# The opening of an attention-and-MLP kernel: halves of 256 queries, silu on GpSimd, and c on another queue

## The chip, the cores and the metric

One NeuronCore of a Trainium2 chip runs the kernel; the other cores are idle. The metric is the device time of one execution in microseconds (us), from ten runs. A profiled execution gives a trace: every engine's instructions with start and duration. The engines are PE (TensorE: matmuls, with weight loads shown apart as PEld), DVE (VectorE), ACT (ScalarE), POOL (GpSimd) and SP (SyncE, which here only issues transfers). A DMA transfer is issued by an instruction in the queue of SP, ACT or POOL, and the data moves on the core's 16 DMA engines. "Bank" is one of the eight 2 KB-per-partition banks of PSUM into which PE writes.

## The reference

The kernel computes one transformer block with adaptive layer norm. With `c` of 512 values, `w_mod` of 512 x 3072, `x` of 2048 x 512, 32 query heads of 128, 8 key/value heads and a window of the last 512 keys:

```
mod = silu(c) @ w_mod                       # six rows of 512: sa, ca, ga, sb, cb, gb
h   = layernorm(x) * (1 + ca) + sa
q   = h @ wq                                # 32 heads of 128
p   = softmax(q @ k[-512:].T / sqrt(128))   # 4 query heads share one k and v head
x   = x + ga * ((p @ v[-512:]) @ wo)
h   = layernorm(x) * (1 + cb) + sb
x   = x + gb * (relu(h @ w1) @ w2)          # w1: 512 x 1792
```

Inputs and output are bfloat16.

## The kernel before

The 2048 queries are taken in four blocks of 512 (QB), each of four tiles of 128 rows. A unit is one head of one block, so there are 128 units. A unit's work on PE is four matmuls for q (K = 512 in four chunks, called cc in the code), four for the scores, sixteen for p times v. ScalarE copies q out of PSUM (line 1493) and takes the exponential of the scores (line 1501); VectorE normalises the result (lines 1511 and 1512). Output projections and, in the end, the MLP fill PE in between.

The order of work on each engine is the order of the calls in the source. A small recorder (`kb.op`) notes for each operation what it reads and writes and works out the semaphore waits; every engine then runs its own list strictly in order. Nothing is scheduled at run time, so an instruction that waits holds up all that stand behind it on its engine or queue.

The change touches only the opening, which prepares the first block (lines 1567 to 1628). It goes like this:

- Transfers (1567 to 1575). SP's queue issues tiles 0 and 1 of x, then c as a 4 x 128 array, the first half of the modulation weights for sa and ca (`wm0`, chunks cc 0 and 1), query weights, keys (with a transposing transfer), values. ScalarE's queue issues tiles 2 and 3 of x, the second half of those weights (`wm1`, chunks 2 and 3), and the query weights of heads 0 and 1.
- GpSimd (1576 to 1581) sets constants and builds the identity matrix for transposes.
- PE (1583 to 1585) runs 7 dummy matmuls on ones (`warm`, into bank psW), transposes c to a column (`silu_exp`, line 1425), and runs 9 more. ScalarE takes exp(-c) from it (1426).
- Layer norm. VectorE takes mean and variance of tiles 0 to 2 (1377, 1378); ScalarE does the same for tile 3 with sums (1587 to 1590). GpSimd raises variance plus epsilon to the power -0.5 for two tiles at a time (`rstd_pow`, 1596). VectorE then finishes the silu in three small steps (`silu_mul`, 1430 to 1432) and normalises tiles 0 to 2 (1388); ScalarE normalises tile 3 (1609, 1610).
- The modulation columns (`mod_cols_mm`, 1434 to 1443): sa and ca are needed with one value per partition, so 32 matmuls with a single moving column give 8 columns of 128 values in bank psQ. They run column by column, the four chunks cc of each in turn, 16 before and 16 after the transposes of tile 0. VectorE copies the columns out, adding 1 to the four of ca, in two operations (1447, 1448).
- PE transposes the other tiles (`ln_tposes`, 1400 to 1404) with 1, 2 and 3 dummy matmuls behind them (1621). All tiles land in two banks, two chunks in each.
- `ln_mod_ps` (1406 to 1418) applies factor and shift, 512 queries at a time: chunks 0 and 1 on VectorE, 2 and 3 on ScalarE. Then q of units 0 and 1 (`q_mms`, 1487 to 1493), into banks psQ and 5, and from there on the steady loop (1657 to 1668).

Two lines that the change replaces, the order of the products and the place where SP gets c:

```
for c2 in range(DC):
    for cc in range(DC):
...
dma(c_row[:, :], c[0].rearrange("(c p) -> c p", p=P), "c", writes=[R_c])
```

Of the kernel before, what the change touches and what calls it, by code (L numbers as in the profile page):

```python
# [1198 lines left out]
def build_fast(nc, es, top, A_x, A_k_cache, A_v_cache, A_wq, A_wo, B_x, B_w1, B_w2, c, w_mod, out, flag):  # L1199
    P = 128  # L1200
    _, Sq, D = A_x.shape
    _, G, Sk, Dh = A_k_cache.shape
# [5 lines left out]
    QB = 512  # L1208
# [3 lines left out]
    DC = D // P  # L1212
# [3 lines left out]
    scale = float(Dh) ** -0.5  # L1216
# [21 lines left out]
    hT = [T(f"hT{i}", [P, DC, QB]) for i in range(2)]  # L1238
# [11 lines left out]
    xn = T("xn", [P, TPB, D])  # L1250
# [5 lines left out]
    ones = T("ones", [P, P])  # L1256
    c_row = T("c_row", [DC, P])
    s3 = T("s3", [P, 4], F32)
    sc_bf = T("sc_bf", [P, DC])
    sc_f = T("sc_f", [P, DC], F32)  # L1260
    tmp = T("tmp", [P, DC], F32)
# [51 lines left out]
    R_moda, R_modb, R_ga, R_gb = Res("moda"), Res("modb"), Res("ga"), Res("gb")  # L1313
    R_pr = [R_ga] + RL("pr", 2) + [R_gb]
    R_st, R_mv, R_rstd = RL("st", NT), RL("mv", NT), RL("rstd", NT)
    R_s3, R_eps = Res("s3"), Res("eps")
    R_rinv, R_vmax, R_chk, R_good, R_flag = Res("rinv"), Res("vmax"), Res("chk"), Res("good"), Res("flag")
    R_h1 = [RL(f"h1_{i}_", FC) for i in range(2)]
# [30 lines left out]
    def wm_res(sl, cc):  # L1349
        return R_wm[cc // (DC // 2)] if sl < 2 else R_wm[sl]  # L1350
# [15 lines left out]
    def mm(out_ap, lhsT, rhs, start, stop, reads, bk, signal):  # L1366
        kb.op(PE, lambda e: e.matmul(out_ap, lhsT, rhs, start=start, stop=stop), reads=reads, group_writes=[R_b[k] for k in bk], signal=signal)  # L1367
# [18 lines left out]
    def ln_norm(t):  # L1386
        b, tl = t // TPB, t % TPB
        kb.op(DVE, lambda e: e.tensor_scalar(xn[:, tl, :], x_sb[:, t, :], mv[:, t, 0:1], rstd[:, t:t + 1], op0=ALU.subtract, op1=ALU.mult),
              reads=[R_x[t], R_mv[t], R_rstd[t]], writes=[R_xn[tl]])
# [9 lines left out]

    def ln_tposes(tl, bks):  # L1400
        for cc in range(DC):
            bk = bks[cc // 2]
# [3 lines left out]
    def ln_mod_ps(bks, dst, R_dst, which):  # L1406
        o, r = (0, R_moda) if which == 1 else (2 * DC, R_modb)
        for k in range(2):
            for half, eng in ((0, DVE), (1, ACT)):
                cc = half * 2 + k  # L1410
                src = bank[bks[half]].bitcast(BF)[:, k * 512:(k + 1) * 512]
                sc, sh = modc[:, o + DC + cc:o + DC + cc + 1], modc[:, o + cc:o + cc + 1]
                if eng is DVE:
                    kb.op(DVE, lambda e, src=src, sc=sc, sh=sh, cc=cc: e.tensor_scalar(dst[:, cc, :], src, sc, sh, op0=ALU.mult, op1=ALU.add),
                          reads=[R_b[bks[half]], r], writes=[R_dst[cc]])
                else:
                    kb.op(ACT, lambda e, src=src, sc=sc, sh=sh, cc=cc: e.activation(dst[:, cc, :], src, ACTF.Identity, bias=sh, scale=sc),
                          reads=[R_b[bks[half]], r], writes=[R_dst[cc]])

    CC_ORDER = (0, 2, 1, 3)  # L1420
    QA = 2

    def silu_exp(bk):
        cT = bank[bk].bitcast(BF)[:, 0:DC]
        kb.op(PE, lambda e: e.transpose(cT, c_row[:, :], ident[0:DC, 0:DC]), reads=[R_c, R_ident], group_writes=[R_b[bk]])
        kb.op(ACT, lambda e: e.activation(tmp[:, :], cT, ACTF.Exp, scale=-1.0), reads=[R_b[bk]], writes=[R_tmp])

    def silu_mul(bk):
        cT = bank[bk].bitcast(BF)[:, 0:DC]
        kb.op(DVE, lambda e: e.tensor_scalar(tmp[:, :], tmp[:, :], 1.0, None, op0=ALU.add), reads=[R_tmp], writes=[R_tmp])  # L1430
        kb.op(DVE, lambda e: e.reciprocal(tmp[:, :], tmp[:, :]), reads=[R_tmp], writes=[R_tmp])  # L1431
        kb.op(DVE, lambda e: e.tensor_tensor(sc_bf[:, :], cT, tmp[:, :], op=ALU.mult), reads=[R_tmp, R_b[bk]], writes=[R_sc])  # L1432

    def mod_cols_mm(which, bk):
        fs = []
        for idx, sl in enumerate((0, 1) if which == 0 else (3, 4)):
            for c2 in range(DC):
                for cc in range(DC):
                    last = idx == 1 and c2 == DC - 1 and cc == DC - 1
                    fs.append(lambda sl=sl, c2=c2, cc=cc, col=idx * DC + c2, last=last: mm(  # L1440
                        bank[bk][:, col:col + 1], wm[sl][:, cc, c2 * P:(c2 + 1) * P], sc_bf[:, cc:cc + 1],
                        cc == 0, cc == DC - 1, [R_sc, wm_res(sl, cc)], [bk], last))
# [43 lines left out]

    def q_mms(u, bk=QBK):
        b, h = units[u]
        order = CC_ORDER if u < QA else range(DC)
        for i, cc in enumerate(order):  # L1490
            mm(bank[bk], wq_sb[:, cc, h * Dh:(h + 1) * Dh], hT[b % 2][:, cc, :], i == 0, i == DC - 1,
               [R_wq[h], R_hT[b % 2][cc]], [bk], i == DC - 1)
# [102 lines left out]
    def rstd_pow(lo, hi):  # L1595
        kb.op(POOL, lambda e: e.tensor_tensor(rstd[:, lo:hi], rstd[:, lo:hi], cst[:, 0:1].to_broadcast([P, hi - lo]), op=ALU.pow),
              reads=R_rstd[lo:hi] + [R_cst], writes=R_rstd[lo:hi])

    ln_stat(0)
    ln_stat(1)  # L1600
    rstd_add(0, 2)
# [8 lines left out]
    kb.op(ACT, lambda e: e.activation(xn[:, t3, :], x_sb[:, t3, :], ACTF.Identity, scale=rstd[:, t3:t3 + 1], bias=s3[:, 3:4]),  # L1610
          reads=[R_x[t3], R_rstd[t3], R_s3], writes=[R_xn[t3]])
# [249 lines left out]
```

## Time and profile before

| What | Value |
|---|---|
| median of 10 runs | 561.61 us (561.34 to 562.2) |
| profiled execution, its own time | 561.49 us |
| its span, first to last instruction | 559.8 us |
| PE busy | 550.1 us, 98% |
| ACT busy | 350.3 us, 63% |
| DVE busy | 252.7 us, 45% |
| POOL busy | 52.1 us, 9% |
| granted TensorE clock | 1.000 |

The profiled execution took 561.49 us, of which 1.69 lie outside the span. In the timeline each row gives the start and the length in us, the engine, the line of the source, the operation, output and input with their shapes, how often, and in square brackets how long the engine had been idle and what ended the idle time. A row with "x16" stands for sixteen instructions of one group and the length covers them all. In the chain of waits each row is one step of the chain that ended last: start, length, engine, tile and line.

The opening's stages in the profile before, each with its start in us:

| Start | Stage |
|---|---|
| 4.74 | first statistics on VectorE, when x has landed (line 1377) |
| 4.75 | weight load for the transpose of c on PE, when c has landed (1425) |
| 8.05 | first normalisation on VectorE (1388) |
| 8.19 | first modulation product on PE |
| 9.41 | modulation columns copied out (1447) |
| 10.75 | factor and shift applied (1414, 1417) |
| 11.44 | first matmul for q |
| 12.68 | q of unit 0 copied out (1493) |
| 13.42 | first matmul for scores |

### The profile page before, as it was taken

How to read it: one execution, taken by the hardware profiler on the slowest of the kernel's cores; microseconds unless marked ns; L12 is line 12 of the kernel's file. 1: busy time of each engine (PE TensorE's matmuls, PEld its weight loads, DVE VectorE, ACT ScalarE, POOL GpSimd, SP SyncE). 2: the span in 40 equal slices, each digit the busy share in tenths (PEclk: the TensorE clock that was granted, in tenths of full speed). 3: DMA queues.
4: the chain of work that ended last, by engine and by line, in shares of the span. 5: the costliest groups of instructions: out<-in, count | busy, mean ns of one | idle time of the engine just before them, and what ended most of it. 6: DMA issues, size and time to landing. Idle time of an engine off the chain costs nothing.

```text
span 559.8 us, 9653 instructions
## 1 busy us (share of the span) xinstructions
PE 550.1 (98%) x4057; PEld 315.0 (56%) x4132; DVE 252.7 (45%) x550; ACT 350.3 (63%) x453; POOL 52.1 (9%) x46
## 2 busy tenths in 40 slices
PE   7999999999999999999999999999999999999998
PEld 3565555555555555555555555555555654444444
DVE  3455555553546544335445443333354448321134
ACT  5986666666666666666666666666666644432500
POOL 1000022004410000033000000332000000000000
PEclk9999999999999999999999999999999999999999
DMA  9896764413214144352452422211214110200001
GB/s 270 238 213 169 144 161 59 114 39 76 40 38 76 39 70 120 57 133 58 94 95 57 75 40 39 38 39 38 39 39 76 39 30 0 45 33 23 21 30 47
DMA packets 113309, 42.67 MB, mean 76 GB/s; under 512 B 93928, under 2 KB 112104, under 8 KB 113256
## 3 DMA queue, kind: packets, MB, share of 16 engines
q1 hardware_dynamic: 112024, 40.82, 34.5%
q10 hardware_dynamic: 1232, 1.15, 0.6%
q8 instruction: 33, 0.54, 0.4%
q14 instruction: 20, 0.16, 0.1%
HBM read 18.35 MB, written 2.10 MB: 37 GB/s over the span
## 4 chain that ended last, share of the span: by engine, by line
PE 97%; issue 1%; DMA 1%; DVE 1%
PE psS L1367 28%; PE psO L1367 27%; PE psQ L1367 23%; PE psW L1367 19%; DMA x<-in_A_x_dram 1%; DVE st L1377 0%; PE psS L1370 0%; DVE mv L1378 0%; DVE rstd L1593 0%; DVE PT L1691 0%; DVE PT L1693 0%; DVE tmp L1431 0%; DVE sc_bf L1432 0%; DVE tmp L1430 0%
## 5 line engine op out<-in xcount | busy, mean ns | idle before, releaser
L1501 ACT ACTIVATE PT<-psS 128x1024 bf16<-128x1024 f32 x256 | 262.7, 1028 | 126.9 <-PE psS L1367 126.9
L1367 PE MATMUL psS<-qT,kT 128*128 128x512 bf16 x510 | 151.4, 379 | 0.1
L1367 PEld LDWEIGHTS psO<-v,PT 128*128 128x128 bf16 x2048 | 126.6, 98 | 30.2
L1367 PE MATMUL psO<-v,PT 128*128 128x129 bf16 x2048 | 137.0, 220 | 0.0
L1367 PE MATMUL psQ<-hT,wq 128*128 128x512 bf16 x505 | 130.2, 379 | 0.2
L1511 DVE RECIPROCAL rinv<-psO 128x4 f32<-128x4 f32 x128 | 23.4, 183 | 229.1 <-PE psO L1367 229.1
L1367 PE MATMUL psW<-wo,oT 128*128 128x512 bf16 x452 | 118.1, 379 | 3.1
L1512 DVE TENSOR_TENSOR o<-psO,rinv 128x512 bf16<-128x512 f32 x128 | 88.5, 691 | 4.7 <-DVE rinv L1511 0.2
L1367 PEld LDWEIGHTS psQ<-hT,wq 128*128 128x128 bf16 x508 | 49.6, 98 | 60.7 <-issue 0.5
L1367 PEld LDWEIGHTS psS<-qT,kT 128*128 128x128 bf16 x512 | 49.5, 98 | 58.9 <-ACT PT L1501 0.7
L1493 ACT ACTIVATE qT<-psQ 128x512 bf16<-128x512 f32 x127 | 75.3, 593 | 0.5 <-PE psQ L1367 0.5
L1680 ACT ACTIVATE wq<-psS 128x512 bf16<-128x512 f32 x56 | 33.4, 597 | 49.4 <-PE psS L1367 49.4
L1367 PEld LDWEIGHTS psW<-wo,oT 128*128 128x128 bf16 x512 | 44.9, 98 | 32.9 <-DVE acc L1534 1.2
L1534 DVE TENSOR_TENSOR acc<-psW,acc 128x512 f32<-128x512 f32 x48 | 33.2, 691 | 6.7 <-PE psW L1367 6.7
L1367 PE MATMUL psO<-wmw,wq 128*128 128x512 bf16 (+1 forms) x164 | 32.7, 352 | 0.3
L1537 POOL TENSOR_TENSOR acc<-acc,gaf 128x512 f32<-128x512 f32 x12 | 15.6, 1303 | 146.8 <-DVE acc L1534 139.7
L1383 POOL TENSOR_TENSOR rstd<-rstd,cst 128x4 f32<-128x4 f32 x7 | 7.2, 1026 | 218.3 <-DVE rstd L1382 218.3
L1691 DVE TENSOR_TENSOR PT<-psO,gbf 128x512 f32<-128x512 f32 (+1 forms) x12 | 7.5, 624 | 40.4 <-PE psO L1367 40.4
L1367 PE MATMUL psS<-h2T,wmw 128*128 128x512 bf16 x110 | 25.2, 379 | 0.1
L1367 PEld LDWEIGHTS psO<-wmw,wq 128*128 128x128 bf16 x168 | 15.4, 98 | 16.5
L1367 PE MATMUL psS<-hT,wmw 128*128 128x512 bf16 x110 | 24.4, 379 | 0.1
L1377 DVE BATCH_NORM_STATS2 st<-x 128x6 f32<-128x512 bf16 x31 | 21.1, 681 | 4.7 <-DMA x<-in_A_x_dram 4.7
(77 smaller groups left out, 189.1 us busy)
## 6 DMA issues: line engine op xcount, KB each, us to landing
wo<-in_A_wo_dram SPq DMA_DIRECT2D x4, 1024.0 KB, 5.8
wq<-in_A_wq_dram SPq DMA_DIRECT2D x7, 512.0 KB, 5.1
wmw<-in_B_w_dram SPq DMA_DIRECT2D x14, 256.0 KB, 3.0
wmw<-in_w_mod_dram SPq DMA_DIRECT2D x5, 512.0 KB, 4.9
oT<-o SPq DMA_TRANSPOSE x128, 2.4
out_dram<-PT SPq DMA_DIRECT2D x15, 128.0 KB, 1.7
x<-in_A_x_dram SPq DMA_DIRECT2D x3, 512.0 KB, 4.6
v<-in_A_v_cache_dram SPq DMA_DIRECT2D x8, 128.0 KB, 4.2
```

The source lines that it names most:

```text
L1367: kb.op(PE, lambda e: e.matmul(out_ap, lhsT, rhs, start=start, stop=stop), reads=reads, group_writes=[R_b[k] for k in bk], signal=signal)
L1377: kb.op(DVE, lambda e: e.bn_stats(st[:, t, :], x_sb[:, t, :]), reads=[R_x[t]], writes=[R_st[t]])
L1383: kb.op(POOL, lambda e: e.tensor_tensor(rstd[:, sl], rstd[:, sl], cst[:, 0:1].to_broadcast([P, hi - lo]), op=ALU.pow), reads=R_rstd[sl] + ...
L1493: kb.op(ACT, lambda e: e.activation(qT[u % NQT][:, :], bank[bk], ACTF.Copy), reads=[R_b[bk]], writes=[R_qT[u % NQT]])
L1501: kb.op(ACT, lambda e: e.activation(PT[u % NPT][:, pr * 2:pr * 2 + 2, :], s_ps[pr][:, :, :], ACTF.Exp, scale=scale), reads=[R_b[pr * 2], R ...
L1511: kb.op(DVE, lambda e: e.reciprocal(rinv[:, u, :], o_ps[:, :, P]), reads=[R_b[5], R_b[6]], writes=[R_rinv])
L1512: kb.op(DVE, lambda e: e.tensor_tensor(o_sb[u % NOS][:, :, :], o_ps[:, :, 0:P], rinv[:, u, :].unsqueeze(2).to_broadcast([P, TPB, P]), op=A ...
L1534: kb.op(DVE, lambda e: e.tensor_tensor(acc[:, tl, :], bank[WBK], acc[:, tl, :], op=ALU.add), reads=[R_b[WBK], R_acc[tl]], writes=[R_acc[tl]])
L1537: kb.op(eng, lambda e: e.tensor_tensor(acc[:, tl, :], acc[:, tl, :], gaf[:, :], op=ALU.mult), reads=[R_acc[tl], R_ga], writes=[R_acc[tl]])
L1680: kb.op(ACT, lambda e: e.activation(h1T[b % 2][:, fc, :], bank[bk], ACTF.Relu), reads=[R_b[bk]], writes=[R_h1[b % 2][fc]], pre=all_events( ...
L1691: kb.op(DVE, lambda e: e.tensor_tensor(yt[i][:, c0:c1], bank[bk][:, c0:c1], gbf[:, c0:c1], op=ALU.mult), reads=[R_b[bk], R_gb], writes=[R_ ...
```

## The change

It does the following, all in the opening:

- c is issued by GpSimd's queue, behind the identity matrix, instead of by SP's.
- The silu moves from VectorE to GpSimd: minimum with 1e38 and plus 1, power -1, times c. As GpSimd doesn't read PSUM here, ScalarE copies the transposed c to SBUF (`c_f`) behind the exponential.
- Tile 3 is normalised by GpSimd in one operation instead of by ScalarE in two. Tile 2 is normalised by VectorE behind the first two tiles and before the modulation columns are copied out.
- The 32 modulation products run by chunk cc, so that the first 16 need only `wm0` and the other 16 only `wm1`. They form a single accumulation in bank psQ. They are copied out by one addition of a constant (`m01`: four zeros, four ones).
- The dummy matmuls behind the transposes of tiles 1 to 3 are gone; those up to the modulation products stay.
- The transposed tiles land in separate banks for tiles 0, 1 and tiles 2, 3 (`TB`). Factor, shift and q of units 0 and 1 are done in halves of 256 queries: five of these passes on VectorE, three on ScalarE.

```diff
@@ order of the modulation products, and their way out
-        for idx, sl in enumerate((0, 1) if which == 0 else (3, 4)):
-            for c2 in range(DC):
-                for cc in range(DC):
...
+        for cc in range(DC):
+            for sl in (0, 1):
+                for c2 in range(DC):
+                    last = sl == 1 and c2 == DC - 1 and cc == DC - 1
...
-        kb.op(DVE, lambda e: e.tensor_copy(modc[:, mo:mo + DC], bank[bk][:, :DC]), reads=[R_b[bk]], writes=[r])
-        kb.op(DVE, lambda e: e.tensor_scalar(modc[:, mo + DC:mo + 2 * DC], bank[bk][:, DC:2 * DC], 1.0, None, op0=ALU.add), reads=[R_b[bk]], writes=[r])
+        kb.op(DVE, lambda e: e.tensor_tensor(modc[:, mo:mo + 2 * DC], bank[bk][:, :2 * DC], m01[:, :], op=ALU.add), reads=[R_b[bk], R_m01], writes=[r])
@@ silu
-    def silu_mul(bk):
-        cT = bank[bk].bitcast(BF)[:, 0:DC]
-        kb.op(DVE, lambda e: e.tensor_scalar(tmp[:, :], tmp[:, :], 1.0, None, op0=ALU.add), reads=[R_tmp], writes=[R_tmp])
-        kb.op(DVE, lambda e: e.reciprocal(tmp[:, :], tmp[:, :]), reads=[R_tmp], writes=[R_tmp])
-        kb.op(DVE, lambda e: e.tensor_tensor(sc_bf[:, :], cT, tmp[:, :], op=ALU.mult), reads=[R_tmp, R_b[bk]], writes=[R_sc])
+        kb.op(ACT, lambda e: e.activation(c_f[:, :], cT, ACTF.Copy), reads=[R_b[bk]], writes=[R_cf])
+
+    def silu_mul():
+        kb.op(POOL, lambda e: e.tensor_scalar(tmp[:, :], tmp[:, :], 1e38, 1.0, op0=ALU.min, op1=ALU.add), reads=[R_tmp], writes=[R_tmp])
+        kb.op(POOL, lambda e: e.tensor_tensor(tmp[:, :], tmp[:, :], cst[:, 3:4].to_broadcast([P, DC]), op=ALU.pow), reads=[R_tmp, R_eps], writes=[R_tmp])
+        kb.op(POOL, lambda e: e.tensor_tensor(sc_bf[:, :], c_f[:, :], tmp[:, :], op=ALU.mult), reads=[R_tmp, R_cf], writes=[R_sc])
@@ transfers and constants
-    dma(c_row[:, :], c[0].rearrange("(c p) -> c p", p=P), "c", writes=[R_c])
     load_wm01(0)
     load_wm01(1, ACT)
...
+    dma(c_row[:, :], c[0].rearrange("(c p) -> c p", p=P), "c", writes=[R_c], eng=POOL)
     kb.op(POOL, lambda e: e.memset(cst[:, 1:2], eps), writes=[R_eps])
+    kb.op(POOL, lambda e: e.memset(cst[:, 3:4], -1.0), writes=[R_eps])
     kb.op(POOL, lambda e: e.memset(v_sb[:, :, :, P:VW], 1.0), writes=[R_v1])
+    kb.op(POOL, lambda e: e.memset(m01[:, 0:DC], 0.0), writes=[R_m01])
+    kb.op(POOL, lambda e: e.memset(m01[:, DC:2 * DC], 1.0), writes=[R_m01])
@@ layer norm of the first block
+    silu_mul()
     ln_stat(0)
     ln_stat(1)
     rstd_add(0, 2)
...
     rstd_pow(2, 4)
-    silu_mul(5)
-    for tl in range(3):
-        ln_norm(tl)
-    kb.op(ACT, lambda e: e.activation(s3[:, 3:4], s3[:, 1:2], ACTF.Copy, scale=rstd[:, t3:t3 + 1]), reads=[R_s3, R_rstd[t3]], writes=[R_s3])
-    kb.op(ACT, lambda e: e.activation(xn[:, t3, :], x_sb[:, t3, :], ACTF.Identity, scale=rstd[:, t3:t3 + 1], bias=s3[:, 3:4]),
+    ln_norm(0)
+    ln_norm(1)
+    kb.op(POOL, lambda e: e.tensor_scalar(xn[:, t3, :], x_sb[:, t3, :], s3[:, 1:2], rstd[:, t3:t3 + 1], op0=ALU.add, op1=ALU.mult),
           reads=[R_x[t3], R_rstd[t3], R_s3], writes=[R_xn[t3]])
+    TB = [[0, 0, 2, 2], [1, 1, 3, 6]]
...
-    ln_tposes(0, [0, 2])
+    ln_tposes(0, TB[0])
     for f in fs[len(fs) // 2:]:
         f()
+    ln_norm(2)
     mod_cols_evac(0, QBK)
@@ halves
-    for tl in range(1, TPB):
-        ln_tposes(tl, [0, 2])
-        warm(tl)
-    ln_mod_ps([0, 2], hT[0], R_hT[0], 1)
+    def mod_half(hf, cc, eng):
+        bk = TB[hf][cc]
+        o = (cc % 2) * 512 + hf * HB
+        src, dst = bank[bk].bitcast(BF)[:, o:o + HB], hT[0][:, cc, hf * HB:(hf + 1) * HB]
...
+    def q_half(u, hf, order, bk):
+        for cc in order:
+            mm(bank[bk][:, hf * HB:(hf + 1) * HB], wq_sb[:, cc, u * Dh:(u + 1) * Dh], hT[0][:, cc, hf * HB:(hf + 1) * HB], cc == CC_ORDER[0], cc == CC_ORDER[-1],
+               [R_wq[u], R_half[hf][cc]], [bk], cc == CC_ORDER[-1])
+
+    for tl in range(1, TPB):
+        ln_tposes(tl, TB[tl // 2])
+    mod_half(0, 0, DVE)
+    mod_half(0, 2, ACT)
+    mod_half(0, 1, DVE)
+    mod_half(0, 3, ACT)
+    q_half(0, 0, CC_ORDER, QBK)
+    mod_half(1, 0, DVE)
+    mod_half(1, 2, ACT)
+    mod_half(1, 1, DVE)
+    mod_half(1, 3, DVE)
+    q_half(1, 0, CC_ORDER, 5)
+    for u, bk in ((0, QBK), (1, 5)):
+        q_half(u, 1, CC_ORDER, bk)
+        q_evac(u, bk)
     load_wq(R, R)
     load_k(1)
     load_v(1)
-    q_mms(0)
-    q_mms(1, 5)
```

More of the change, by code (lines that the diff above doesn't have):

```diff
@@ L1258, in build_fast @@
     s3 = T("s3", [P, 4], F32)
+    c_f = T("c_f", [P, DC], F32)
+    m01 = T("m01", [P, 2 * DC], F32)
     sc_bf = T("sc_bf", [P, DC])
@@ L1315, in build_fast @@
     R_st, R_mv, R_rstd = RL("st", NT), RL("mv", NT), RL("rstd", NT)
+    R_h0 = RL("h0", DC)
+    R_cf, R_m01 = Res("cf"), Res("m01")
     R_s3, R_eps = Res("s3"), Res("eps")
@@ L1401, in ln_tposes @@
         for cc in range(DC):
-            bk = bks[cc // 2]
+            bk = bks[cc]
             o = (cc % 2) * 512 + tl * P
             tpose(bank[bk].bitcast(BF)[:, o:o + P], xn[:, tl, cc * P:(cc + 1) * P], [R_xn[tl]], [bk], cc == DC - 1)
[L1406 to L1418, printed above, removed]
     CC_ORDER = (0, 2, 1, 3)
@@ L1426, in silu_exp @@
         kb.op(ACT, lambda e: e.activation(tmp[:, :], cT, ACTF.Exp, scale=-1.0), reads=[R_b[bk]], writes=[R_tmp])
-    def silu_mul(bk):
-        cT = bank[bk].bitcast(BF)[:, 0:DC]
-        kb.op(DVE, lambda e: e.tensor_scalar(tmp[:, :], tmp[:, :], 1.0, None, op0=ALU.add), reads=[R_tmp], writes=[R_tmp])
-        kb.op(DVE, lambda e: e.reciprocal(tmp[:, :], tmp[:, :]), reads=[R_tmp], writes=[R_tmp])
-        kb.op(DVE, lambda e: e.tensor_tensor(sc_bf[:, :], cT, tmp[:, :], op=ALU.mult), reads=[R_tmp, R_b[bk]], writes=[R_sc])
+        kb.op(ACT, lambda e: e.activation(c_f[:, :], cT, ACTF.Copy), reads=[R_b[bk]], writes=[R_cf])
[3 more added lines that the diff above has]
+        kb.op(POOL, lambda e: e.tensor_tensor(sc_bf[:, :], c_f[:, :], tmp[:, :], op=ALU.mult), reads=[R_tmp, R_cf], writes=[R_sc])
     def mod_cols_mm(which, bk):
         fs = []
-        for idx, sl in enumerate((0, 1) if which == 0 else (3, 4)):
-            for c2 in range(DC):
-                for cc in range(DC):
-                    last = idx == 1 and c2 == DC - 1 and cc == DC - 1
-                    fs.append(lambda sl=sl, c2=c2, cc=cc, col=idx * DC + c2, last=last: mm(
+        for cc in range(DC):
+            for sl in (0, 1):
+                for c2 in range(DC):
+                    last = sl == 1 and c2 == DC - 1 and cc == DC - 1
+                    fs.append(lambda sl=sl, c2=c2, cc=cc, col=sl * DC + c2, last=last: mm(
                         bank[bk][:, col:col + 1], wm[sl][:, cc, c2 * P:(c2 + 1) * P], sc_bf[:, cc:cc + 1],
-                        cc == 0, cc == DC - 1, [R_sc, wm_res(sl, cc)], [bk], last))
+                        cc == 0 and sl == 0 and c2 == 0, last, [R_sc, wm_res(sl, cc)], [bk], last))
         return fs
@@ L1488, in q_mms, with q_evac @@
         b, h = units[u]
-        order = CC_ORDER if u < QA else range(DC)
-        for i, cc in enumerate(order):
+        for i, cc in enumerate(range(DC)):
             mm(bank[bk], wq_sb[:, cc, h * Dh:(h + 1) * Dh], hT[b % 2][:, cc, :], i == 0, i == DC - 1,
-               [R_wq[h], R_hT[b % 2][cc]], [bk], i == DC - 1)
+               [R_wq[h], R_hT[b % 2][cc]] + ([R_h0[cc]] if b == 0 else []), [bk], i == DC - 1)
+        q_evac(u, bk)
+    def q_evac(u, bk=QBK):
         kb.op(ACT, lambda e: e.activation(qT[u % NQT][:, :], bank[bk], ACTF.Copy), reads=[R_b[bk]], writes=[R_qT[u % NQT]])
@@ L1614, in build_fast @@
         f()
-    ln_tposes(0, [0, 2])
+    ln_tposes(0, TB[0])
     for f in fs[len(fs) // 2:]:
         f()
+    ln_norm(2)
     mod_cols_evac(0, QBK)
-    for tl in range(1, TPB):
-        ln_tposes(tl, [0, 2])
-        warm(tl)
-    ln_mod_ps([0, 2], hT[0], R_hT[0], 1)
+    HB = QB // 2
+    R_half = [R_h0, R_hT[0]]
+    def mod_half(hf, cc, eng):
+        bk = TB[hf][cc]
+        o = (cc % 2) * 512 + hf * HB
+        src, dst = bank[bk].bitcast(BF)[:, o:o + HB], hT[0][:, cc, hf * HB:(hf + 1) * HB]
+        sc, sh = modc[:, DC + cc:DC + cc + 1], modc[:, cc:cc + 1]
+        if eng is DVE:
+            kb.op(DVE, lambda e: e.tensor_scalar(dst, src, sc, sh, op0=ALU.mult, op1=ALU.add), reads=[R_b[bk], R_moda], writes=[R_half[hf][cc]])
+        else:
+            kb.op(ACT, lambda e: e.activation(dst, src, ACTF.Identity, bias=sh, scale=sc), reads=[R_b[bk], R_moda], writes=[R_half[hf][cc]])
+    def q_half(u, hf, order, bk):
+        for cc in order:
+            mm(bank[bk][:, hf * HB:(hf + 1) * HB], wq_sb[:, cc, u * Dh:(u + 1) * Dh], hT[0][:, cc, hf * HB:(hf + 1) * HB], cc == CC_ORDER[0], cc == CC_ORDER[-1],
+               [R_wq[u], R_half[hf][cc]], [bk], cc == CC_ORDER[-1])
+    for tl in range(1, TPB):
+        ln_tposes(tl, TB[tl // 2])
[11 more added lines that the diff above has]
+        q_half(u, 1, CC_ORDER, bk)
+        q_evac(u, bk)
     load_wq(R, R)
```

## The prediction, made before the changed kernel ran

> **What bounds the kernel now.** I read the page's totals first, then its chain of waits, then the opening instruction by instruction.
>
> ```profile
> span 559.8 us, 9653 instructions
> PE 550.1 (98%) x4057; PEld 315.0 (56%) x4132; DVE 252.7 (45%) x550; ACT 350.3 (63%) x453; POOL 52.1 (9%) x46
> ...
> PE 97%; issue 1%; DMA 1%; DVE 1%
> ```
>
> From about 13.4 us on, TensorE never rests: 97% of the chain is PE. A change that touches only the opening can move the time only by moving the start of that stretch, and everything behind slides along. So the number to predict is when the first query reaches ScalarE's evacuation (line 1493, at 12.68) and so when the first score matmul starts (13.42). The chain through the opening, in order of time:
>
> ```profile
> 7.65 0.09 DVE tmp L1430
> ...
> 7.97 0.17 DVE sc_bf L1432
> ...
> 8.19 0.55 PE psQ L1367 x16
> 8.75 0.24 PE psS L1370 x4
> 8.99 0.38 PE psQ L1367 x16
> ...
> 10.05 0.43 PE psW L1367 x2
> 10.49 0.22 PE psS L1370 x4
> 10.71 0.65 PE psW L1367 x3
> ```
>
> Three things to see: the silu's three tiny DVE steps stand in front of everything (7.57 to 8.13); dummy matmuls (psW) stand between the transposes; and the last transposes start only at 10.33. Next, the timeline rows that price the parts:
>
> ```profile
> 6.74 0.72 POOL L1596 TENSOR_TENSOR rstd<-rstd,cst 128x2 f32<-128x2 f32 x1 [4.83 <-DVE rstd L1593]
> 7.73 0.76 POOL L1596 TENSOR_TENSOR rstd<-rstd,cst 128x2 f32<-128x2 f32 x1 [0.27 <-DVE tmp L1430]
> ...
> 128.21 1.69 POOL L1537 TENSOR_TENSOR acc<-acc,gaf 128x512 f32<-128x512 f32 x1 [31.07 <-DVE acc L1534]
> ...
> 147.43 1.26 POOL L1537 TENSOR_TENSOR acc<-acc,gaf 128x512 f32<-128x512 f32 x1 [7.05 <-issue]
> ```
> ```profile
> 8.05 1.05 DVE L1388 TENSOR_SCALAR xn<-x,mv,rstd 128x512 bf16<-128x512 bf16 x3
> ...
> 10.75 0.99 DVE L1414 TENSOR_SCALAR hT<-psS,modc 128x512 bf16<-128x512 bf16 x2 [0.98 <-PE psS L1370]
> ```
> ```profile
> 8.86 0.81 ACT L1610 ACTIVATE xn<-x,s,rstd 128x512 bf16<-128x512 bf16 x1
> 10.75 1.45 ACT L1417 ACTIVATE hT<-psS,modc 128x512 bf16<-128x512 bf16 x2 [1.08 <-PE psS L1370]
> ```
>
> And the transfers, the wait that c's landing ended (timeline) and the modulation weights' time from issue to landing (last column, us):
>
> ```profile
> 4.75 0.09 PEld L1425 LDWEIGHTS psO<-ident,c_row 4*128 4x128 bf16 x1 [1.45 <-DMA c_row<-in_c_dram]
> ```
> ```profile
> wmw<-in_w_mod_dram ACTq DMA_DIRECT2D x1, 512.0 KB, 4.9
> wmw<-in_w_mod_dram SPq DMA_DIRECT2D x1, 512.0 KB, 6.2
> ```
>
> **Silu on GpSimd.** DVE loses three operations; its first normalisation moves from 8.05 to 7.67, right behind line 1593 (end 7.65), if rstd(0,2) is there. GpSimd gets three operations of 128x4. The pow has a row of its shape (line 1383, 1.03 us). The clamp-and-add and the product have none: at least a memset (0.10), at most the 128x2 pow (0.74). I take 0.2, nearest to the memset and to the 128x128 select (0.29). With 0.07 between neighbours (line 1537 ends at 151.16, line 1538 starts at 151.23): 0.2+1.03+0.2+3x0.07=1.64, bounds 1.4 to 2.7. The exponential ends at 5.13, so the silu is ready at 6.8 instead of 8.13 (6.6 to 7.9). Queued behind it on GpSimd are rstd(0,2), until now at 6.74, then rstd(2,4), then the new xn(3). 6.8+0.75 gives 7.55, just early enough for 7.67; rstd(2,4) still goes at 7.75 to 8.51, since it needs line 1593. So there is practically no slack: what delays the silu by more than 0.1 us delays all of this one for one. ScalarE's extra copy of c (0.17, the exponential's row) pushes line 1590 from 7.16 to 7.33, hidden before 7.75.
>
> **c through the GpSimd queue.** c's issue on SP (0.36 us at 1.24) goes, so every later SP transfer is issued 0.42 us sooner: the modulation weights of SP took 6.2 us from 1.66, landing at 7.86, so about 7.45 now (7.86 at worst). ScalarE's half landed at 6.1. The first 16 products then take 0.4 to 0.55 us and end about 8.0, under the wait for xn(0) at 8.08; at worst this costs 0.2. c itself was issued at 1.24 and ended PE's wait at 4.75, 3.5 us. On GpSimd it is issued behind the select, at 1.61. No transfer of this queue is in the trace. From the rows: shortest landing 1.4 us (the 32 KB store), longest in the opening 7.3 us (query weights on ScalarE's queue), so 3.0 to 8.9. SP's packets of x ran until 3.5 and c stood behind them; the new queue is empty, but its setup is unknown. I take 3.1 us, which lands at 4.7 as today, and keep both ends. The memsets now behind c on GpSimd (eps, -1, ones of v, the constant) are not needed before 5.2; that cover is 3.3 us.
>
> The Trainium skill, "DMA: Bandwidth & Descriptors", section "Latency and other measured facts", gives about 1 µs to the first byte for a transfer set up by GpSimd and 0.6 for one of SP; no row here shows it. By it alone c would land at 1.61+3.5+0.4=5.5, and the sum would be 0.65 worse than mine.
>
> **Last tile's normalisation on GpSimd.** ScalarE's 0.29+0.81 (8.53 to 9.67) go. One GpSimd pass of 128x512 bf16 has no row: at least two 128x256 memsets (0.62), at most line 1538 (1.16). I take 0.9: 8.58 to 9.48. DVE does xn(2) at the same time (8.55 to 8.95). Line 1537 warns here: at 128.21 it took 1.69, beside a DVE operation that ran until 128.78, against 1.27 in the other rows. So an overlap can cost GpSimd 0.42; yet DVE's first normalisation at 8.05 ran at full speed inside the pow at 7.73. I take no collision, and keep 0.42 on GpSimd or 0.85 on DVE as the other end.
>
> The Trainium skill speaks against this part: "SBUF — State Buffer", section "Who interferes with whom", says that a VectorE tensor_scalar in a two-port mode and a GpSimd operation lock each other out for the whole instruction. By that rule one of the two waits; the gain would be about 1.0 (GpSimd waits) or 0.6 (DVE waits) instead of 1.45.
>
> **PE.** xn(0) at 8.08, transposes 8.14 to 8.38, the other 16 products to 8.95 (0.38 on the chain, then the drain), one 0.16 pass instead of two (9.41 to 9.76): the factors are there at 9.15, not 9.76. Transposes of tiles 1 and 2 follow to 9.25 with no dummies; tile 3, on xn(3), 9.54 to 9.92 (0.38, its row) instead of 10.71. The dummies removed are 6x0.215. Without them PE's gaps stay under 0.6 us; the 1.2 us before 8.19 already did not slow the 0.215 us matmuls after it.
>
> **Halves.** A 256-wide DVE pass: 0.54 (row) less half of what is above a tiny operation's 0.16, 0.35, and 0.26 apart (0.45 less 0.19). ScalarE: 0.77 becomes 0.47. First half 9.2 to 9.8 on DVE, to 10.1 on ScalarE, under the wait for tile 3. Second half from 9.94: three on DVE, 2x0.26+0.35=0.87, to 10.81; ScalarE's one to 10.57. Of unit 0 only one 256-wide matmul remains then. Before, 0.43 passed from its start to the evacuation (12.25 to 12.68), now 0.32: evacuation at 11.2. **Sum:** 12.68-11.2=1.48, 1.45 with rounding: 0.8 from the earlier last transposes, the rest from halving.
>
> It is kept: first use of each load now against its landing is 9.9 against 9.0 (wq0), 11.9 against 9.7 (k0), 12.4 against 9.2 (wq2), 15.5 against 10.4 (v0), 16.7 against 11.9 (wq4). The profiled execution took 561.49, 1.69 outside its span, 0.12 under the median: 561.49-1.45=560.04, or 560.2 against the median of 561.61.
>
> **Rivals.** *GpSimd is too slow* (collision, or xn(3) at 1.16, or small operations near 0.5): 0.42 to 0.85 of 1.45 lost, 560.6 to 561.0. For it: line 1537's 1.69. Against: 8.05. *c arrives late*: the place is PE's transpose at 1425; ScalarE's statistics of tile 3 stand behind the exponential and three GpSimd steps behind the silu, so lateness counts in full beyond 4.85. From a landing at 6.3 it is slower than before; at the upper end, 8.9, 4.05-1.45=2.6 are lost: 564.2. For it: no row shows this queue; loads in this stretch took up to 7.3. Against: c is 1 KB on an empty queue. *The start is earlier but not the end*, a load or ScalarE's 63% taking it back behind 13 us: 561.5. For it: ScalarE's waits for scores are only 126.9 of 560; against: the landings above and PE at 97%.
>
> **Numbers.** Forecast 0.58, its own range 559.8 to 560.5; slow GpSimd 0.20; late c 0.14 (mostly 562 to 564.2); nothing kept 0.08. A measurement can tell 0.2%, 1.12 us: faster means under 560.49, slower over 562.73. Faster: 0.56 of the forecast plus 0.03 of the second, 0.59; slower: 0.13 of late c; the rest, 0.28, within. Low end: xn(3) at 0.62, about 0.15 less than 560.2, and as much for gaps: 559.8. High end 561.9 takes in all but the late landings.
>
> **What will show it.** c's wait ending at 4.2 to 5; sc_bf at about 6.8; xn(3) on GpSimd of 0.6 to 1.2 ending near 9.5; factors at 9.2; last transposes at 9.5 to 9.9; first evacuation of a query at 11.2, first scores near 11.95; an unchanged stretch behind. Wrong, if c ends PE's wait after 5.5, or if xn(2) and xn(3) run one after the other.

## The result and the profile after

| | Before | After |
|---|---|---|
| median | 561.48 us (561.18 to 562.46, 28 runs) | 564.49 us (563.84 to 565.35, 8 runs) |
| ratio to before, 95% interval | | 1.0053 (1.0044 to 1.0061) |
| profiled execution, and its span | 561.49, 559.8 us | 564.76, 563.0 us |

The change costs 3.0 us. That lies outside the predicted range (559.8 to 561.9). What happened is the rival "c arrives late"; the time is 0.3 us above the upper end of 564.2 that the prediction gave this rival. The page of the profile after begins as follows: totals, the head of the chain of waits, and in between the queue that is new.

```profile
span 563.0 us, 9664 instructions
...
PE 550.4 (98%) x4060; PEld 315.9 (56%) x4134; DVE 253.1 (45%) x549; ACT 349.3 (62%) x453; POOL 55.6 (10%) x54
...
q0 software_dynamic: 32, 0.00, 0.0%
...
PE 97%; DMA 1%; issue 1%; DVE 0%; ACT 0%; POOL 0%; POOLq 0%; DVEq 0%
```

PE's work is as before (550.4 against 550.1 us), but the span has grown by 3.2: PE began its long stretch later. The chain of waits of the kernel after shows where. Its rows are start, length, what:

```profile
1.33 0.26 POOL ident L1568
1.59 6.51 DMA c_row<-in_c_dram
...
8.14 0.18 PE psO L1415
8.32 3.79 PE psW L1371 x9
12.11 0.38 PE psQ L1371 x16
12.49 0.25 PE psS L1374 x4
12.74 0.39 PE psQ L1371 x16
13.15 0.18 DVE modc L1437
...
13.44 0.42 DVE hT L1623
...
13.99 0.78 PE psQ L1371 x4
14.77 0.44 PE psO L1371 x4
15.21 0.45 PE psQ L1371 x4
...
15.68 0.61 ACT qT L1484
```

Before, the silu on VectorE and the dummies between the transposes led this chain. Now c itself leads it, with 6.51 us from issue to landing, and behind it the nine dummy matmuls with 3.79 us. The first query is copied out at 15.68 instead of 12.68, the first score matmul starts at 16.64 instead of 13.42: 3.0 and 3.2 us later. The end of the span has moved by 3.2, the median by 3.0. In the timeline of the kernel after, the rows that answer to those of the prediction:

```profile
1.59 0.85 POOL L1303 DMA_DIRECT2D c_row<-in_c_dram  x1
...
8.14 0.10 PEld L1415 LDWEIGHTS psO<-ident,c_row 4*128 4x128 bf16 x1 [4.82 <-DMA c_row<-in_c_dram]
...
8.25 3.86 PE L1371 MATMUL psW<-ones 128*128 128x512 bf16 x9
...
8.48 0.63 ACT L1581 ACTIVATE xn<-x 128x512 bf16<-128x512 bf16 x1
8.63 0.28 POOL L1420 TENSOR_SCALAR tmp<-tmp 128x4 f32<-128x4 f32 x1 [5.46 <-ACT c_f L1417]
...
8.99 1.05 POOL L1421 TENSOR_TENSOR tmp<-tmp,cst 128x4 f32<-128x4 f32 x1
...
10.12 0.20 POOL L1422 TENSOR_TENSOR sc_bf<-c_f,tmp 128x4 bf16<-128x4 f32 x1
...
11.02 1.22 DVE L1392 TENSOR_SCALAR xn<-x,mv,rstd 128x512 bf16<-128x512 bf16 x3 [3.38 <-POOL rstd L1590]
...
11.90 0.90 POOL L1603 TENSOR_SCALAR xn<-x,s,rstd 128x512 bf16<-128x512 bf16 x1
11.95 0.54 PE L1371 MATMUL psQ<-sc_bf,wmw 128*128 128x1 bf16 x16
```

PE's wait for c ended at 4.75 before and ends at 8.14 here. Everything that stands behind c slid with it: ScalarE's statistics of tile 3 (8.48, in line behind the exponential), GpSimd's powers for the layer norm (in line behind the silu, so VectorE waited 3.38 us for them), and with those the normalisations. The second thing to see is the row with x9: nine dummies take 3.86 us here and 2.13 where nothing disturbs them. That is 0.43 us for each, against the 0.215 that the prediction took from the kernel before.

What held c up? The queues of the kernel after between 3.5 and 5.5 us, and then between 5.5 and 8 (packets, MB, share of the 16 DMA engines; q1 carries SP's transfers, q10 ScalarE's, q0 is GpSimd's queue):

```profile
q1 hardware_dynamic: 237, 0.46, 62.4%
q10 hardware_dynamic: 159, 0.29, 39.0%
```
```profile
q10 hardware_dynamic: 561, 0.49, 58.9%
q1 hardware_dynamic: 629, 0.36, 47.1%
q0 software_dynamic: 32, 0.00, 0.8%
```

c was issued from 1.59 to 2.44, but not one of its 32 packets moved before 5.5. From 3.5 to 5.5 the 16 engines were full (62.4 and 39.0%) with what had been issued ahead of it: the last of x, and the 1 MB of modulation weights issued at 1.24. That is a reading, not yet a proof: GpSimd's queue might also just be slow. The experiments separate the two.

### The profile page after: what moved, and what is told of

Same layout as the page of the kernel before. It is cut to its first block, busy times and chain, and to the rows that moved or that the text cites. A ratio compares the mean times of both kernels' runs of the same rounds, so it can differ in the third digit from the quotient of the medians.

```text
span 563.0 us, 9664 instructions
## 1 busy us (share of the span) xinstructions
PE 550.4 (98%) x4060; PEld 315.9 (56%) x4134; DVE 253.1 (45%) x549; ACT 349.3 (62%) x453; POOL 55.6 (10%) x54
## 4 chain that ended last, share of the span: by engine, by line
PE 97%; DMA 1%; issue 1%; DVE 0%; ACT 0%; POOL 0%; POOLq 0%; DVEq 0%
PE psS L1371 28%; PE psO L1371 26%; PE psQ L1371 23%; PE psW L1371 20%; DMA c_row<-in_c_dram 1%; ACT qT L1484 0%; DVE hT L1623 0%; DVE PT L1713 0%; DVE PT L1715 0%; POOL ident L1568 0%; PE psS L1374 0%; POOL ones L1566 0%; PE psO L1415 0%; DVE modc L1437 0%; POOL cst L1567 0%
## 5 line engine op out<-in xcount | busy, mean ns | idle before, releaser
L1371 PE MATMUL psQ<-hT,wq 128*128 128x512 bf16 (+1 forms) x510 | 130.5, 377 | 0.3 <-DVE hT L1623 0.2
```

## The experiments

Theory A says that c waits in the shared DMA engines behind the bulk issued before it. Theory B says that GpSimd's queue itself takes some 6 us. A second question is what the dummies' slow clock costs, a third what the rest of the change is worth. Each kernel's time is given beside the kernel before in the same comparison.

**c back on SP, the rest of the change kept.**

```diff
+    dma(c_row[:, :], c[0].rearrange("(c p) -> c p", p=P), "c", writes=[R_c])
     load_wm01(0)
...
-    dma(c_row[:, :], c[0].rearrange("(c p) -> c p", p=P), "c", writes=[R_c], eng=POOL)
```

> The changed kernel with only c put back on SP's queue, between x and the modulation weights. Theory (late c is the whole loss): c ends PE's wait at about 4.75 again, the 9 dummies take about 2.1 us, the modulation columns leave PSUM near 9.2, the first query is evacuated near 11.7 (13.15 to 15.68 is 2.5 us in the changed kernel), so 560.5 us, 560.1 to 560.9. Rival (the rest of the change loses too, through GpSimd's slow small steps or the halves): 561.5 or more, first evacuation at 12.7 or later.

Measured: 560.66 us against 561.37, ratio 0.9987 (0.9978 to 0.9996). The 3.8 us between this and the kernel after are the price of c's place, the slow dummies included. But of the 1.45 us forecast for the rest only 0.7 are there. Its timeline:

```profile
4.66 0.18 PE L1415 MATMUL psO<-ident,c_row 4*128 4x4 bf16 x1 [0.44 <-DMA c_row<-in_c_dram]
...
6.63 0.20 POOL L1422 TENSOR_TENSOR sc_bf<-c_f,tmp 128x4 bf16<-128x4 f32 x1
...
8.22 0.54 PE L1371 MATMUL psQ<-sc_bf,wmw 128*128 128x1 bf16 x16 [1.05 <-DMA wmw<-in_w_mod_dram]
...
9.42 0.17 DVE L1437 TENSOR_TENSOR modc<-psQ,m 128x8 f32<-128x8 f32 x1 [0.23 <-PE psQ L1371]
...
11.95 0.60 ACT L1484 ACTIVATE qT<-psQ 128x512 bf16<-128x512 f32 x1 [0.79 <-PE psQ L1371]
```

The silu is ready at 6.83, as forecast, but the products wait until 8.22 for SP's half of the modulation weights (6.43 us from issue to landing in its chain of waits). A new wait stands where the silu stood. x, too, landed later in this profile (first statistics at 4.97, at 4.74 before), and tile 3 was normalised by 9.76, just before its transposes; so earlier weights alone would hardly have brought those transposes forward.

**Only c's move, on the kernel before.**

```diff
-    dma(c_row[:, :], c[0].rearrange("(c p) -> c p", p=P), "c", writes=[R_c])
...
+    dma(c_row[:, :], c[0].rearrange("(c p) -> c p", p=P), "c", writes=[R_c], eng=POOL)
```

> The kernel before with one edit, c issued by GpSimd's queue behind the identity matrix. Theory (c's route alone loses): c lands near 8.1, ScalarE's statistics of tile 3 and the 9 dummies slide behind it, the dummies run at 0.42 us each, the first query is evacuated near 16.6 instead of 12.68, so about 565.4 us, 564.3 to 566. Rival (c is late only in company with the other edits, e.g. because the modulation weights are issued earlier): c lands before 6 and the time stays under 562.5.

Measured: 565.69 us against 561.37, ratio 1.0074 (1.0058 to 1.0089). Its timeline:

```profile
7.80 0.18 PE L1425 MATMUL psO<-ident,c_row 4*128 4x4 bf16 x1 [3.58 <-DMA c_row<-in_c_dram]
...
7.92 4.02 PE L1367 MATMUL psW<-ones 128*128 128x512 bf16 x9
...
16.86 0.60 ACT L1493 ACTIVATE qT<-psQ 128x512 bf16<-128x512 f32 x1 [0.48 <-PE psQ L1367]
```

c ends PE's wait at 7.80, the nine dummies take 4.02 us, the first query is out at 16.86. This one line costs 4.3 us by itself; the other parts of the change won back 1.2.

**c as GpSimd's first instruction.**

```diff
+    dma(c_row[:, :], c[0].rearrange("(c p) -> c p", p=P), "c", writes=[R_c], eng=POOL)
     for i in range(2):
...
-    dma(c_row[:, :], c[0].rearrange("(c p) -> c p", p=P), "c", writes=[R_c], eng=POOL)
```

> The changed kernel with c's issue as GpSimd's first instruction, some 0.8 us earlier, so that its descriptors are out before those of the modulation weights. Theory A (c waits in the DMA engines behind the bulk that was issued before it): with only x ahead it lands at 4.5 to 5.5 and the time is 560.5 to 561.3. Theory B (a transfer of this queue takes about 6.5 us whatever is ahead): it lands near 7.3, the time is 563.4 to 564. A landing in between would be a mixture.

Measured: 563.17 us against 561.37, ratio 1.0035 (1.0022 to 1.0048); c landed at 7.3. It decides little: the issue began at 1.31, only 0.28 earlier than in the kernel after, and takes GpSimd 0.85 us, so it still ended at 2.16, after the weights had been issued (1.24 to 1.70). Both theories can live with 7.3. It ran better than the kernel after for two reasons. c landed 0.8 us earlier (7.3 for 8.1). And the constants behind c came later, the seven dummies started only at 2.45 instead of 1.06, PE's gap was shorter, and the nine behind c took 2.13.

**The weights wait until c has landed.** Nothing but x is then ahead of c. All that stands behind the weights on the two queues waits with them, so the bulk is not only issued later than c but absent until c has landed. The weights are late in exchange, so the time says nothing; c's landing is what counts.

```diff
-        dma(wm01[:, c0:c1, :], wm01v[:, c0:c1, :], f"wm{i}", writes=[R_wm[i]], eng=eng)
+        kb.op(eng or SP, lambda e: e.dma_start(wm01[:, c0:c1, :], wm01v[:, c0:c1, :]), writes=[R_wm[i]], pre=[(dsem("c"), 16)], dma_sem=dsem(f"wm{i}"))
```

> The changed kernel, c on GpSimd's queue where it stands, but both transfers of the modulation weights (1 MB) wait until c has landed. Only x is ahead of c then. It tells why c took 6.0 to 6.5 us there. Theory A (its packets stood behind the bulk in the DMA engines): c's packets start soon after x's last ones at 3.5 and it lands at 4.3 to 5.5, that is 2.7 to 3.9 us after its issue at 1.58. Theory B (the queue itself takes 6 us): it lands at 7.6 or later. The time as such says little, since the weights come late: some 566 us by A, 569 by B.

Its chain of waits has c, with the weights' issue behind it, and the queues between 2.5 and 4.5 us show c's packets:

```profile
1.58 3.51 DMA c_row<-in_c_dram
...
5.11 0.46 ACTq L1351
```
```profile
q10 hardware_dynamic: 119, 0.21, 27.5%
q1 hardware_dynamic: 100, 0.17, 24.8%
q0 software_dynamic: 31, 0.00, 0.8%
```

The same transfer on the same queue takes 3.51 us instead of 6.51, and 31 of its 32 packets move before 4.5. Theory B falls: the queue alone isn't slow. (565.22 us in one run; its start is set by the late query weights, and from 11 to 18 us the granted clock was about 0.5.)

**c on SP, but behind SP's half of the weights.** The opposite test: the old queue, and the bulk ahead.

```diff
     load_wm01(0)
+    dma(c_row[:, :], c[0].rearrange("(c p) -> c p", p=P), "c", writes=[R_c])
     load_wm01(1, ACT)
...
-    dma(c_row[:, :], c[0].rearrange("(c p) -> c p", p=P), "c", writes=[R_c], eng=POOL)
```

> The changed kernel with c on SP's queue, not GpSimd's, but issued behind SP's half of the modulation weights instead of ahead of it. Theory A (the bulk ahead makes c late, whatever queue it is on): c ends PE's wait at 6.5 to 8, and the time is 562.5 to 564.5 us, about as slow as the changed kernel. Theory B (it is GpSimd's queue): c lands by 5.2 and the time is under 561.2 us.

Measured: 563.33 us against 561.58, ratio 1.0035 (1.0022 to 1.0049). Its chain of waits:

```profile
1.71 5.18 DMA c_row<-in_c_dram
...
6.94 0.18 PE psO L1415
7.12 3.71 PE psW L1371 x9
```

On SP, too, 1 KB behind the weights takes 5.18 us. Here c stands behind them in one and the same queue, so this run says nothing of one queue holding up another; that is shown by the run before it. The two together: the bulk makes c late, behind it on SP's queue and beside it on GpSimd's. GpSimd's queue adds something under that load, 0.4 to 1.2 us (landings at 7.3 to 8.1 against 6.9); with nothing but x ahead it added nothing that shows (3.51 us, against 3.5 on SP before).

That the engines are full does not by itself hold up a small transfer. In the kernel before, c on SP's queue landed 3.5 us after its issue at 1.24, although ScalarE's half of the weights, issued at 1.23, held 96% of the engines from 4.0 to 4.5. No run has c on GpSimd's queue fully issued ahead of the bulk and the bulk in flight behind it. So whether the order of issue decides on that queue, or any bulk in flight, stays open.

**More dummies ahead of c: 23, then 18, instead of 7.** They fill PE's gap, to see what the slow clock costs.

```diff
-    warm(7)
+    warm(23)
```

> The changed kernel with 23 instead of 7 dummy matmuls ahead of c's transpose, so that PE doesn't rest for 3.9 us while c is late. Theory (PE lost its clock in that gap: 9 dummies took 3.86 us instead of 2.13): the 9 take about 2.0 again, the transposes of tile 0 start near 11.5 instead of 12.35, and the time is 0.6 to 0.8 lower than the changed kernel, about 563.8 us. Rival (the dummies were not what held the chain, GpSimd's steps were): 564.3 to 564.7, no different from the changed kernel.

Measured: 564.48 us against 561.37, ratio 1.0054 (1.0041 to 1.0068), a miss. The nine dummies took 2.13 us as hoped, but 23 were too many: they held PE until 8.95, some 1 us after c had landed (7.8: issued at 1.58, 6.2 us to landing), and c's transpose started at 8.96. What the clock gave, the overshoot took. So, with 18:

```diff
-    warm(7)
+    warm(18)
```

> As the run with 23 dummies, but with 18 in place of 7 ahead of c's transpose, so that they end about when c lands (23 ended at 8.95, 0.9 after it). Theory (PE's clock, lost in the gap, costs time of its own): the 9 dummies behind take 2.1 us, the first query is evacuated near 14.8 instead of 15.68, the time is 563.6 us, 0.8 under the changed kernel. Rival (nothing gained, c's chain through GpSimd sets it): 564.4, evacuation at 15.5 or later.

Measured: 563.79 us against 561.54, ratio 1.0054 (1.0035 to 1.0072). These are four runs, one of them at 566.13, and the ratio is not that of the two medians (1.0040). By time alone it can't be told from the kernel after. By stage it can; the timeline of this kernel:

```profile
7.95 0.09 PEld L1415 LDWEIGHTS psO<-ident,c_row 4*128 4x128 bf16 x1 [1.42 <-DMA c_row<-in_c_dram]
...
8.06 2.13 PE L1371 MATMUL psW<-ones 128*128 128x512 bf16 x9
...
14.64 0.60 ACT L1484 ACTIVATE qT<-psQ 128x512 bf16<-128x512 f32 x1 [0.79 <-PE psQ L1371]
```

c comes 0.19 us earlier than in the kernel after, and the first query 1.04 us earlier. The other 0.85 are the clock's.

**ScalarE's half of the products first, with c on SP.** That half of the weights lands first, so the wait that the first experiment found should go. Edited from that kernel:

```diff
-        for cc in range(DC):
+        for cc in (2, 3, 0, 1):
...
```

> c on SP's queue as in the first run, and the 16 products of chunks 2 and 3 (weights from ScalarE's queue, landed at 6.3) ahead of those of chunks 0 and 1 (landed at 8.06, PE waited for them). Theory (that wait holds the chain): the first 16 products start near 7.2 instead of 8.22, the transposes of tile 0 follow xn(0) at once, the columns are out 0.1 to 0.2 earlier: 560.3 to 560.6 us. Rival (tile 3's normalisation on GpSimd and the passes behind it set the end): 560.66 as in the first run, the evacuation unmoved against the first statistics.

Measured: 560.43 us against 561.54, ratio 0.9979 (0.9970 to 0.9988). This is the lowest median of all, 1.1 us under the kernel before. But the execution that was profiled is the slowest of its eleven (561.48), and shows why it was slow:

```profile
4.87 0.18 PE L1415 MATMUL psO<-ident,c_row 4*128 4x4 bf16 x1 [0.65 <-DMA c_row<-in_c_dram]
...
4.98 3.96 PE L1371 MATMUL psW<-ones 128*128 128x512 bf16 x9
```

The nine dummies ran at half speed and held the products until 8.77, although PE had paused for only 0.65 us. So this profile doesn't show the earlier products that the theory asked for; the next one does.

**Nine dummies ahead of c and five behind it**, so that PE is busy earlier and fewer stand in the way of the products:

```diff
-    warm(7)
+    warm(9)
     silu_exp(5)
-    warm(9)
+    warm(5)
```

> c on SP's queue, ScalarE's half of the products first, and the dummies split 9 ahead of c's transpose and 5 behind it instead of 7 and 9. In the run with ScalarE's half first the 9 dummies ran cold in the profiled execution (3.96 us, to 8.9) and held the products. Theory (the clock at that point differs from one execution to the next, and a gap of 0.65 us before c is enough to lose it): PE is busy from 1.0 to 4.9 without a gap, the 5 dummies take 1.1 to 2.1 us and end by 7.2, the first products start at 7.2 or earlier, the time is 559.9 to 560.3 us. Rival (the split doesn't matter, tile 3 sets the end): 560.4 us.

Measured: 560.61 us against 561.58, ratio 0.9991 (0.9982 to 1.0000). A miss: no better than the last. The profiled execution is the fastest of the eleven (560.36):

```profile
7.17 0.55 PE L1371 MATMUL psQ<-sc_bf,wmw 128*128 128x1 bf16 x16 [0.86 <-POOL sc_bf L1422]
...
11.62 0.60 ACT L1484 ACTIVATE qT<-psQ 128x512 bf16<-128x512 f32 x1 [0.79 <-PE psQ L1371]
```

The products start at 7.17, but then the layer norm of tile 0 (8.28) and tile 3 on GpSimd (8.69 to 9.59) set the path. The eleven executions fall into two groups. Six read a granted clock of 1.000 and took 560.36 to 560.61 us; five read 0.997 and took 561.35 to 561.79. In the run before this one all eleven read 1.000. So with the new split PE lost part of its clock in some executions; where and why is not shown.

**Without the halves, with c on SP** (512 queries at a time again).

```diff
-        for i, cc in enumerate(range(DC)):
+        for i, cc in enumerate(CC_ORDER if u < QA else range(DC)):
...
-        ln_tposes(tl, TB[tl // 2])
...
+        ln_tposes(tl, TB[0])
+    ln_mod_ps([0, 2], hT[0], R_hT[0], 1)
...
+    q_mms(0)
+    q_mms(1, 5)
```

> c on SP's queue as in the first run, and factor, shift and q again 512 queries wide, as in the kernel before; all else of the change stays. Theory (halving is worth what the prediction gave it, 0.65 us): the first query is evacuated 0.65 later, 12.6, and the time is 561.3 us. Rival (halving is worth 0.2 or less, because five VectorE passes of 0.40 us each replace two of 0.54): evacuation near 12.15, 560.9 us or less.

Measured: 561.04 us against 561.54, ratio 0.9988 (0.9979 to 0.9997), against 0.9987 with the halves. The difference of the two is known to some 0.7 us only, so the forecast 0.65 for halving is neither confirmed nor excluded. Its profiled execution (563.01, 2 us over its own median) can't be compared stage by stage: SP's weights landed 0.8 later than in the first experiment, and behind a pause of 2.2 us on PE the granted clock was 0.50 from 11 to 14 us.

**Silu on VectorE again, with c on SP.**

```diff
-    silu_mul()
     ln_stat(0)
...
     rstd_pow(2, 4)
+    silu_mul(5)
     ln_norm(0)
```

> c on SP's queue as in the first run, and the silu back on VectorE in three operations (ScalarE's copy of c gone with it); all else of the change stays. Theory (the silu's place was worth the 0.4 us by which VectorE's first normalisation moved): the first normalisation starts 0.4 to 0.5 later after the first statistics (3.3 instead of 2.8), the evacuation 0.3 to 0.5 later, 561.0 us. Rival (the silu's place is worth nothing, since in the first run PE waited for the weights until 8.22 in any case): evacuation within 0.15, 560.7 us.

Measured: 560.86 us against 561.58, ratio 0.9986 (0.9977 to 0.9995): the same as with the silu on GpSimd. In its profile x and the weights landed earlier (first statistics at 4.51 for 4.97, SP's half at 7.6 for 8.1), and the silu, not the weights, let the products go at 7.96. Counted from the first statistics, VectorE's first normalisation starts 3.31 us after them, 2.82 in the first experiment, and the first query is out after 7.19 for 6.98: 0.2 later, between the two forecasts. Where the silu runs is worth 0.2 us by these profiles, and nothing that the medians can tell.

## Why the prediction was wrong, and where it was right

**The step that failed** is "c through the GpSimd queue": "I take 3.1 us, which lands at 4.7 as today", with the reason "SP's packets of x ran until 3.5 and c stood behind them; the new queue is empty". Measured were 6.51 us and 8.1, and with them came the sign of being wrong that the prediction had named, c ending PE's wait after 5.5. The queue was empty, but the 16 engines behind it were not: on SP c had been issued ahead of SP's half of the weights, on GpSimd it came behind both halves. The prediction had the row that says so (ScalarE's query weights, issued behind others in this stretch, took 7.3 us) and used it only as the upper bound. The argument "c is 1 KB on an empty queue" was the mistake: it asked what stands ahead of c in its own queue, and not what else the engines had to move.

The Trainium skill, "DMA: Bandwidth & Descriptors", section "Issuing engines are not separate DMA queues" and the rules at its end, says that SP, ScalarE and GpSimd all feed the same 16 engines, whose transfers interleave. c on GpSimd's queue agrees with the first half: 6.51 us beside the other queues' weights, 3.51 without them. Whoever takes the second half to mean that 1 KB gets through early doesn't find it here: none of its packets moved before 5.5. With the page's 1 µs to the first byte for GpSimd (section "Latency and other measured facts") the prediction's estimate was a landing at 5.5; 8.1 was measured.

**A term that the prediction left out** is the clock. "Without them PE's gaps stay under 0.6 us" was said of the early c; with the late one PE stood still from 4.2 to 8.1, and the dummies that follow ran at 0.43 us each. How much of it counts shows in one table: from c's transpose to the first query out, in the kernel before and in the profiles in which c leads the path. (In the kernel before, x's statistics and the silu behind them lead it.)

| Kernel | c's transpose | first query out | between | the nine dummies |
|---|---|---|---|---|
| before | 4.75 | 12.68 | 7.93 | 2.13 |
| after | 8.14 | 15.68 | 7.54 | 3.86 |
| c behind the weights on SP | 6.94 | 14.40 | 7.46 | 3.78 |
| ScalarE's half first | 4.87 | 12.51 | 7.64 | 3.96 |
| c first on GpSimd | 7.35 | 14.03 | 6.68 | 2.13 |
| 23 dummies | 8.96 | 15.64 | 6.68 | 2.13 |
| 18 dummies | 7.95 | 14.64 | 6.69 | 2.13 |
| nine and five dummies | 4.94 | 11.62 | 6.68 | (five in 1.26) |

Where the dummies run at full speed, the changed opening takes 6.68 us from c on, four times over; where they run at half speed, 7.46 to 7.64, each time 3.68 more than the nine dummies themselves. So the 3.0 us come apart: c late by 8.14-4.75=3.39, the clock 7.54-6.69=0.85, and the rest of the change gains 7.93-6.69=1.24. 3.39+0.85-1.24=3.00. That the three close is so by construction; what the runs show is that 6.68 comes back. The clock's part rests on profiles; the medians of the kernels with 7 and with 18 dummies lie 0.7 us apart, within their scatter.

**The price of a late c** was right in kind: the prediction's "what delays the silu delays all of this one for one" shows in ScalarE's and GpSimd's rows above. By its formula a landing at 8.09 gives (8.09-4.85)-1.45=1.8 us; 3.0 were measured. Of the difference 0.85 are the clock, 0.2 the smaller gain of the rest (1.24 for 1.45), and 0.15 come from counting the lateness from 4.85.

**The sum for the rest of the change** (1.45) was too large: 1.24 where c leads the path, 0.7 in the medians with c on SP. The term that was mis-sized is the stretch behind the last transposes, from their end to the first query: 11.2-9.92=1.28 in the prediction. With nine and five dummies, where c leads and no weights are waited for, the last transposes end 5.10 us after c's transpose (10.04), which is sooner than the 5.17 of the prediction, but from there to the first query it takes 1.58. The prediction let VectorE's passes over the second half set this stretch and left one 256-wide matmul of unit 0. In the chain of waits PE sets it: twelve 256-wide matmuls in a row from 10.04 to 11.60 (0.67, 0.44 and 0.45 for four each), four of them unit 1's, which stand ahead of unit 0's second half. The first four take longer because the last of them waits for ScalarE's second pass over the first half, which ends at 10.37; so these passes were not hidden "under the wait for tile 3" either.

With c on SP, a second difference is the landing of SP's weights. The "about 7.45 now (7.86 at worst)" was meant for SP's queue without c. In the kernel after they landed at 7.15 (issued at 1.25, 5.9 us) and ScalarE's half at 7.7 (where 6.1 was kept), and neither held PE, which was still at its dummies. In the first experiment, c ahead of them again, they landed at 8.09 and did hold the products. There the prediction's 11.2 for the first query became 11.95: 0.29 from the later end of the last transposes (10.21 for 9.92), 0.46 from the stretch behind them. With ScalarE's half first the gain is 1.1 in the medians. The passes themselves were a little longer than taken: 1.37 for four on VectorE, 0.40 for a single one (taken 0.35), 0.49 each on ScalarE (taken 0.47).

**What held.** The silu's three operations took 0.28, 1.05 and 0.20 (taken 0.2, 1.03, 0.2), ready at 6.83 for 6.8 in the first experiment. Tile 3's pass took 0.90, exactly the value taken. No collision with VectorE showed: VectorE's normalisations kept 0.41 beside it, and it kept 0.90 beside them (0.98 in the kernel with the silu on VectorE). So the rival "GpSimd is too slow" did not happen, nor did the lock-out that the prediction weighed beside it. The columns leave in one pass of 0.17. Behind the opening nothing changed, as said: the shift of 3.2 at the first scores is the shift at the end of the span.

## What to carry to other kernels

An empty queue is not an empty DMA engine. A small transfer that starts a chain was early here on a queue where it stood ahead of the bulk, and late behind the bulk on the same queue or beside it on GpSimd's; that one moved line cost over three times what all other parts of the change won. Before taking work off a path, look for the load that comes next on it; here it was the weights at 8.1, and taking the products of the half that lands first brought the median from 0.7 to 1.1 us under the kernel before (the two intervals overlap, so this step is not proven). And a late arrival in front of PE is to be priced twice, once as waiting and once as slow matmuls afterwards.

## What the runs showed of the hardware

- 1 KB issued from GpSimd behind 1 MB issued on two other queues took 6.0 to 6.5 us, and 3.5 with only x (512 KB) ahead. On SP it took 3.5 us ahead of SP's half, with ScalarE's half issued at the same moment, and 5.18 behind SP's half. What in the engines orders them so, and why GpSimd's queue loses another 0.4 to 1.2 us under load only, stays open.
- Issuing c kept GpSimd busy for 0.85 us, SP for 0.36 to 0.41. Work behind such an issue on GpSimd waits for it: in the kernel with c first, PE's dummies, which need GpSimd's constants, started at 2.45 instead of 1.06.
- In the profile of the kernel after the granted clock reads 1.000 throughout, also over the 3.86 us in which nine matmuls ran at half speed; there the loss is seen only in the spacing of the matmuls. Two profiles do show it in the clock: without the halves (0.50 from 11 to 14 us, after a pause of 2.2 us) and with the weights waiting for c (about 0.5 from 11 to 18, after a pause of 3.0).
- After pauses of 2.7 to 3.9 us the nine dummies were slow each time (3.78 to 4.02 us). After pauses of 0.9 to 1.8 us they were not in any of three kernels (2.13). After pauses of 0.4 to 0.7 us, with 3.2 us of dummies before them, they were in one kernel (3.96), partly in another (2.40) and not in three more (2.13). The Trainium skill, "TensorE: Matmul & The Clock Gate", "Part 1", tells of a window of 3.4 µs that runs freely, so that the moment of the switch varies from execution to execution. These rows fit it, though no run here shows the window itself.
